# Single maxima of a two-branch attention kernel, spread over all steps by a running share

## The chip, the cores and the metric

The kernel runs on one core of a Trainium2 chip. The metric is device time in microseconds (us) of one execution, the median of several runs.

## The reference

Two attention branches over one input x (2048 rows, 512 columns), mixed row by row by a sigmoid gate:

```python
g = sigmoid((x * gate_w).sum(-1, keepdims=True))
a = A(x, wqkv, wo_a)      # 32 heads of 16; each row sees 8 rows: itself, 2, 4, .. 14 before
b = B(x, wq, wk, wv, wo_b)   # 32 heads of 16, one shared key and value head, all 2048 rows
return g * a + (1 - g) * b

# B, for each head: scores = q @ k.T / 4 ; p = softmax(scores) ; o = p @ v
```

The weights `B_wq` and `B_wk` are drawn eight times larger than the others, so B's scores are large, and its softmax needs the maximum of each row of scores before the exponential.

## The kernel before, in words

**Branch B** bounds the kernel. Its 32 *units* are 4 blocks of 512 query rows times 8 groups of 4 heads. A unit has 16 *steps*, one for each 128 keys, so there are 512 attention steps (`NS`). Step `s` takes four score matmuls on TensorE, in two pairs (`exp_pair`, line 569; a pair uses the upper and the lower 64 rows of the array side by side), into two PSUM buffers of two banks each, `pe0` and `pe1`. ScalarE takes the exponential of each buffer (line 571, `pexp`). One step later four matmuls multiply the exponentials with the values (`weighted`, line 579) and add up in the bank `po`.

The exponential needs the row maximum. It is subtracted inside the score matmul: two extra rows of the stacked queries `qst` hold it. So each unit's **maxima** must be known before its first step: 64 tasks a unit, each a score matmul with the queries as stationary side and 512 keys as moving side, and a reduction over them. There are 2048 such tasks (`NF`). They are taken in three ways:

- a *pair* (`fill_pair`): two matmuls side by side into the two-bank buffer `m2` (named `pm`), and one VectorE reduction of 1024 values (line 414). Most steps take one pair, between their two pairs of scores.
- a *single* (`fill_one`): one matmul into the bank `m1` (named `ps`), and one VectorE reduction of 512 values (line 425). A step takes at most one, and none in the first step of most units. The rule `singles` decides.
- *halves* (`fill_diff`, `fill_sum`, line 481): four maxima at once from sum and difference of two blocks of keys, with four matmuls, two absolute values on ScalarE and two fused reductions on VectorE (line 524). They are taken only where TensorE streams a projection on the other half of its rows.

`to_go()` is the number of maxima still to take. A finished unit of maxima goes through `filled`, `maxima_turn`, `shift_a` to `shift_d`: one closing reduction and a transpose on VectorE, small products, and eight small DMAs into `qst`. Units of queries are loaded into `qst` (`stack`) when a buffer comes free, so maxima can be taken only some units ahead: `stacked` lists the units loaded, and `home(v)[1]` is the unit that must be over before unit `v` can be loaded.

**The front** comes before the attention steps: the input's split into high and low parts, keys, queries, and branch A's projection in 48 pieces (line 1190). Maxima are taken along the way, in the end as halves.

**Branch A** runs on GpSimd (POOL) beside the attention steps, by a generator (`work`) that the planner feeds.

**Output rows** (branch A's and B's products with `wo_a`, `wo_b`) are made in two *output phases* (`out_phase`, line 863) of 8 and 4 rows between attention steps, each at the second step of a unit, with halves beside the products. The second phase starts when the lead in maxima falls under three units. The last 4 rows' products (line 934) are spread over the last steps (`spread`), once at most 9 maxima are left to take. They use `m2`, so no pairs go beside them.

**The order** of all this is fixed when the program is built. A planner in the kernel's own code keeps a clock for each engine (`clk`), due times of the banks (`free`) and a list of tasks, and writes the instructions in the order that comes out. Within a step the order is: first scores, pair, then second scores and single, or single and second scores where the planner thinks that the second score buffer is still held, then the weighted products.

Of the kernel before, what the change touches and what calls it, by code (L numbers as in the profile page):

```python
# [18 lines left out]
NJ = S // P  # L19
# [5 lines left out]
NU = NQB * NHG  # L25
# [10 lines left out]
NB = 8  # L36
NS = NU * NJ
NF = 2 * NU * 2 * 4 * 4
FMAX = 3.4028234e38
NH = NJ // 2  # L40
TO_END = 10
LAND = 3
LEAD, M2S, M1S, E1S, PER_ROW = 3.0, 0.5, 0.3, 0.2, 21
M2H = 0.15
WB = 6
# [33 lines left out]
def gated_mix_kernel(ctx, tc, xt, wa, wk, wq, wo_a, wo_b, out):  # L79
# [21 lines left out]
    def home(v):  # L101

        return (v % NB, v - NB) if v < 2 * NB - 2 else ((v - NB) % (NB - 2), v - NB + 2)
# [241 lines left out]
    stacked, asked = [], set()  # L345

    def stack(u):
        qb, hg = divmod(u, NHG)
        for b in range(2):
            hi, lo = (qd[s, :, qb, 4 * hg + 2 * b:4 * hg + 2 * b + 2, :].rearrange("d c n -> d (c n)") for s in range(2))  # L350
            ap = [list(x) for x in hi.ap]
            twice = bass.AP(tensor=hi.tensor, offset=hi.offset, ap=[ap[0], [0, 2]] + ap[1:])
            dst = qst[home(u)[0]].rearrange("p c n -> p (c n)").bitcast(F32)
            nc.sync.dma_start(dst[64 * b:64 * b + 32], twice)
            nc.sync.dma_start(dst[64 * b + 32:64 * b + 48], lo)
        stacked.append(clk["pe"] + 5.0)


    mx, left = {}, {}
    slots = [(v, pr, t, kc) for kc in range(2) for v in range(2) for pr in range(2) for t in range(4)]  # L360
    slots += [(v, pr, t, kc) for v in range(2) for pr in range(2) for t in range(4) for kc in range(2, 4)]
    slots += [(v, pr, t, kc) for v in range(2, NU) for pr in range(2) for t in range(4) for kc in range(4)]
    half = []
# [4 lines left out]
    def fillable():  # L368
        return bool(half) or bool(slots) and slots[0][0] < len(stacked) and stacked[slots[0][0]] <= clk["pe"]
# [17 lines left out]
    def to_go():  # L387
        return 2 * len(slots) + len(half)
# [41 lines left out]
    sel, kcd, dd, formed, ended, wants = [], [], [], set(), set(), []  # L430
# [40 lines left out]
    def half_back():  # L471

        nc.sync.dma_start(q67.rearrange("p g x n -> p (g x n)").bitcast(F32), kd.rearrange("p g x n -> p (g x n)"))
        kcd[0] = q67

    def paired():
        return len(slots) > 1 and slots[0][3] % 2 == 0 and slots[0][3] // 2 in formed and slots[1] == slots[0][:3] + (slots[0][3] + 1,) and fillable()
# [5 lines left out]
    groups, pend, half_free = [], [[], []], [0.0, 0.0]  # L483

    def diff_ready(odd):

        if max(half_free) != free["m2"]:
            half_free[:] = [free["m2"]] * 2
        if half_free[odd] > clk["pe"] or clk["dve"] - 1.6 > clk["pe"]:
            return False  # L490
        mine = [g for g in groups if odd in g[2]]
        if not mine and (groups or half or ended or wants or not paired()):
            return False
        d = mine[0][1] if mine else dd[0]
        return all(x[1] is not d for x in pend[odd])
# [66 lines left out]
    pe, pexp, exped = [], {}, {}  # L562
# [174 lines left out]
    def prepare(j, n, copy=None):  # L737
        nonlocal pool
        hi, lo = turned[j, 1] = [pe[0].tile([P, C, P], F32R, name=f"own{x}", bufs=1) for x in range(2)]
        own = ob[j // 4][:, :n, j % 4 * P:(j % 4 + 1) * P]  # L740
        if copy:
            copy(hi[:, :n], own)
            at = max(clk["pe"], pool / 1e3) + 1.3
        else:
            nc.scalar.activation(hi[:, :n], own, AF.Copy)
            at = after("act", clk["pe"], 0.6)
        nc.gpsimd.tensor_sub(lo[:, :n], own, hi[:, :n].bitcast(F32))
        pool = max(pool, 1e3 * at) + 1300
# [25 lines left out]
    def blocks_out(j):  # L774

        own = p2[0].tile([P, D], F32, name="raw", bufs=1)
        for k in range(2):
            nc.vector.transpose(own[:, k * D // 2:(k + 1) * D // 2], oa[k][:, j, :])
        after("dve", 0, 0.9)
        tasks.append((clk["dve"] + 0.3, blocks_in, (j, own)))  # L780
# [191 lines left out]

    def singles(s):

        if len(stacked) < NU:
            ready = len(half) + 2 * sum(x[0] < len(stacked) for x in slots[:16 * NB])
            if ready < 2 * (16 * (home(len(stacked))[1] + 1) + LAND - s) + 1:
                return False
        return 2 * max(0, 16 * (NU - 1) - 16 - s) + PER_ROW * max(0, NJ - 4 - outs) < to_go()

    def fill_ready(key, slack):
        if fillable() and free[key] <= clk["pe"] + slack:
            clk["pe"] = max(clk["pe"], free[key])
            if key == "m1":
                fill_one()
            elif half and (not slots or slots[0][0] >= len(stacked) or stacked[slots[0][0]] > clk["pe"]):
                fill_one(m2[:, 0, :], "m2")
            elif slots:
                fill_pair(m2, "m2")

    def pause(most):
        n = 0
        while n < most and slots and fillable():
            key = min(("e0", "e1", "m2"), key=lambda k: free[k])
            clk["pe"] = max(clk["pe"], free[key])
            if half:
                fill_one({"e0": eb[0], "e1": eb[1], "m2": m2}[key][:, 0, :], key)
                n += 1
                continue
            fill_pair({"e0": eb[0], "e1": eb[1], "m2": m2}[key], key)  # L1000
            n += 2
        return n
# [28 lines left out]
    def run_tasks():  # L1031
        for task in [t for t in tasks if t[0] <= clk["pe"]]:
            tasks.remove(task)
            task[1](*task[2])
# [207 lines left out]
    outs, due = 0, []  # L1242
    for s in range(NS + 1):
        u, kt = divmod(s, NJ)
        if s == 16 * NB + 4:
            half_back()
        if len(stacked) < NU and s >= 16 * (home(len(stacked))[1] + 1):
            stack(len(stacked))
        if s < NS and kt == 0 and u not in shifted:
            while u not in shifted:  # L1250
                clk["pe"] += 0.5
                run_tasks()
                if u not in shifted and left.get(u, 1):
                    assert pause(4)
        v = min(x[0][0] for x in (half, slots, [(NU,)]) if x)
        need = left.get(v, NF // NU)
        steps = 16 * v - 6 - s
        short = need - 2.8 * max(0, steps) if v < NU else 0
        lead = (NF - to_go()) / 64 - s / 16
        order = (0, "m2", "later") if s else ()  # L1260
        rows = 4 if outs else 8
        k, n = (outs + rows) // 4 - 1, C - (outs >= NJ - 4)
        if outs == NJ - 4:
            if s in (16 * NU - 40, 16 * NU - 32):
                blocks_out(outs + (s - 16 * NU + 40) // 8)
            if to_go() <= 9 and not later_rows and "last" not in done:
                later_rows.append(spread(list(range(outs, NJ)), n))
            if short > 0 and steps < 2:
                pause(short)
        elif due or outs < NJ and s and kt == 0 and outs // NH in done and NHG * (k + 1) - 1 in shaped and (lead < LEAD or s >= 16 * (NHG * (k + 2) + 1)):  # L1270
            if not due:
                prepare(outs, n)
                due.append(n)
            else:
                out_phase(list(range(outs, outs + rows)), due.pop(), kt == 1)
                outs += rows
                order = (0, "m1", 2)
        elif short > 0 and steps < 2:
            pause(short)

        first = 0
        some = min(4, -(-(row_prods[0] - TO_END) // (NS + 1 - s)))
        order = list(order)
        while order:
            which = order.pop(0)
            if which == "later":
                order = ["m1", 1] if free["e1"] > clk["pe"] - E1S else [1, "m1"]
                first = 0
            elif which == "m2":
                fill_ready("m2", M2S)  # L1290
            elif which == "m1":
                if not later_rows and (kt or not s or u >= NU - 8) and singles(s):
                    first = half[0][4] if half else 0
                    fill_ready("m1", M1S)
            elif s < NS:
                if which == 1:
                    spread_some(some)
                exp_pair(s, which % 2 or which // 2, which == 2, first)
        if s == NS:
            spread_some(some)  # L1300
        if s:
            weighted(s - 1)
            if kt == 0 and s < NS:
                finish_a(u - 1, nc.gpsimd)
        run_tasks()
        run_pool()
# [65 lines left out]
```

## Time and profile before

| what | value |
| --- | --- |
| time, median of 3 runs | 1473.9 us (1473.9 to 1474.03) |
| the profiled execution | 1473.35 us, span 1471.6 us |
| granted TensorE clock | 1.000 |
| front (until the first exponential of an attention step) | 268.65 us |
| singles in the front, in the attention steps (line 425) | 50, 374 |
| pairs (line 414) | 506 |
| steps 0 to 15, 176 to 191, 432 to 447 | 32.87, 33.82, 32.15 us |

The span runs from the first to the last instruction; the execution's time is a little longer. An exponential in a step starts ScalarE's row of line 571, so the steps' starts can be read from them. A busy time of TensorE is modelled from the starts of pipelined matmuls, so it reads as full also where an instruction waits a little between two others.

### The profile page before, as it was taken

To read this page: it belongs to the slowest core of one execution; us is meant where nothing else is said; L and a number is where in the kernel's file an instruction comes from. 1 tells how busy PE (TensorE), PEld (TensorE's weight loads), DVE (VectorE), ACT (ScalarE), POOL (GpSimd) and SP (SyncE) were. 2 spreads that over 40 slices of the span, in tenths; PEclk is the share of its full clock that TensorE was granted. 3 is DMA by queue.
4 is the path that set the end of the run, shared out by engine and by line. 5 is a ranking of instruction groups with operands and counts; after the bars stand their busy time and mean duration, and the time that the engine had idled before them with its cause. 6 is when DMAs were issued, how large, how long until landed. Compare 5 with 4: busy or idle time off the path is not lost.

```text
span 1471.6 us, 28990 instructions
## 1 busy us (share of the span) xinstructions
PE 1461.3 (99%) x10612; PEld 669.0 (45%) x10612; DVE 1189.9 (81%) x1865; ACT 1288.7 (88%) x1629; POOL 1003.5 (68%) x1753
## 2 busy tenths in 40 slices
PE   9999999999999999999999999999999999999998
PEld 5877777433333333333333376333333336433343
DVE  6978889688888988889898888889898887766612
ACT  5658888999999999999999978999999998999986
POOL 7853888878898988888888888788888213101221
PEclk9999999999999999999999999999999999999999
DMA  6752533222121110211211202021120000000110
GB/s 224 211 162 74 147 92 100 74 56 77 29 88 42 45 65 36 71 42 42 71 41 41 82 23 86 22 72 42 42 71 12 12 13 26 16 1 2 29 32 29
DMA packets 75263, 89.80 MB, mean 61 GB/s; under 512 B 56368, under 2 KB 56416, under 8 KB 70896
## 3 DMA queue, kind: packets, MB, share of 16 engines
q1 hardware_dynamic: 68176, 49.00, 11.8%
q0 software_dynamic: 6368, 37.90, 7.8%
q8 instruction: 83, 1.36, 0.4%
q10 hardware_dynamic: 576, 1.05, 0.2%
q14 instruction: 60, 0.49, 0.1%
HBM read 60.03 MB, written 27.35 MB: 59 GB/s over the span
## 4 chain that ended last, share of the span: by engine, by line
PE 95%; DVE 2%; POOL 1%; issue 1%; ACT 1%; DVEq 0%; POOLq 0%; ACTq 0%
PE po L579 35%; PE pe L569 24%; PE pe L1190 10%; PE pm L385 8%; PE ps L385 6%; PE pe L863 4%; PE pm L481 2%; PE ps L481 2%; PE po L481 2%; PE pm L934 1%; PE pe L209 1%; DVE qst L187 0%; POOL wal L113 0%; DVE pexp L524 0%; POOL qlo L255 0%
## 5 line engine op out<-in xcount | busy, mean ns | idle before, releaser
L571 ACT ACTIVATE pexp<-pe 128x1024 f32<-128x1024 f32 x1022 | 989.8, 1022 | 84.5 <-PE pe L569 78.9
L414 DVE TENSOR_REDUCE mx<-pm 128x2 f32<-128x1024 f32 x506 | 619.1, 1223 | 152.1 <-PE pm L385 147.4
L579 PE MATMUL po<-pexp,vst 128*32 128x512 f32 x4096 | 545.5, 605 | 0.0
L569 PE MATMUL pe<-qst,kst 64*128 64x512 f32 x1916 | 440.4, 453 | 0.2
L569 PEld LDWEIGHTS pe<-qst,kst 64*128 64x128 f32 x1916 | 179.7, 183 | 482.2 <-ACT pexp L571 477.1
L425 DVE TENSOR_REDUCE mx<-ps 128x1 f32<-128x512 f32 x399 | 271.5, 680 | 0.6 <-PE ps L385 0.6
L385 PE MATMUL pm<-kst,qst 62*128 62x512 f32 x978 | 196.8, 395 | 0.3 <-DVE mx L414 0.3
L643 POOL TENSOR_TENSOR pr<-aext 128x256 f32<-128x256 f32 x256 | 182.8, 741 | 4.7 <-DMA aext<-ad 4.4
L703 POOL TENSOR_TENSOR oa<-oa,av 128x256 f32<-128x256 f32 x224 | 164.4, 734 | 14.9
L579 PEld LDWEIGHTS po<-pexp,vst 128*32 128x32 f32 x4096 | 80.5, 108 | 169.2 <-issue 160.7
L385 PE MATMUL ps<-kst,qst 62*128 62x512 f32 x397 | 157.2, 396 | 0.2 <-DVE mx L425 0.2
L700 POOL TENSOR_TENSOR av<-aext,lg 128x256 f32<-128x256 f32 x224 | 139.6, 623 | 12.9
L507 ACT ACTIVATE dd<-pm 128x512 f32<-128x512 f32 x186 | 105.0, 606 | 23.2 <-PE pm L481 15.3
L1190 PE MATMUL pe<-wah,xh 64*128 64x512 f32 x376 | 119.9, 397 | 0.1
L1190 PE MATMUL pe<-wal,xh 64*128 64x512 f32 x376 | 118.4, 395 | 0.8 <-POOL wal L113 0.8
L1190 PE MATMUL pe<-wah,xl 64*128 64x512 f32 x376 | 118.8, 395 | 0.0
L385 PEld LDWEIGHTS pm<-kst,qst 62*128 62x128 f32 x978 | 94.3, 187 | 2.9 <-DVE mx L414 0.9
L606 POOL TENSOR_TENSOR rl<-rl,gate_t 128x16 f32<-128x16 f32 x31 | 6.9, 223 | 128.0 <-DVE rl L600 126.8
L649 POOL TENSOR_TENSOR tr<-pr 128x512 f32<-128x512 f32 x64 | 81.8, 1278 | 4.2
L507 ACT ACTIVATE pexp<-pm 128x512 f32<-128x512 f32 x120 | 68.5, 608 | 14.5 <-PE pm L481 8.2
L649 POOL TENSOR_TENSOR tr<-tr 128x256 f32<-128x256 f32 (+1 forms) x128 | 72.6, 567 | 8.7
L524 DVE CUSTOM_DVE_ANT_0 dd<-ps,dd 128x512 f32<-128x512 f32 x93 | 64.2, 690 | 15.8 <-PE ps L481 8.7
(214 smaller groups left out, 1983.3 us busy)
## 6 DMA issues: line engine op xcount, KB each, us to landing
aext<-ad POOLq DMA_DIRECT2D x32, 1056.0 KB, 5.5
qst<-qd SPq DMA_DIRECT2D x60, 128.0 KB
ad<-stage SPq DMA_DIRECT2D x32, 240.0 KB
xraw<-xt SPq DMA_DIRECT2D x16, 256.0 KB
qd<-qhi SPq DMA_DIRECT2D x16, 256.0 KB
qd<-qlo SPq DMA_DIRECT2D x16, 256.0 KB
qst<-qd SPq DMA_DIRECT2D x60, 64.0 KB
qst<-ml SPq DMA_DIRECT2D x216, 2.0 KB
```

Of the source, the lines that this page charges most:

```text
L385: nc.tensor.matmul(dst, qst[home(v)[0]][b:b + 62, pr, t * P:(t + 1) * P], kst[b:b + 62, kc * 512:(kc + 1) * 512], start=True, stop=True)
L414: nc.vector.tensor_reduce(m[:, :, pr, t, kc], dst, AX.X, ALU.max)
L425: nc.vector.tensor_reduce(m[:, odd, pr, t, kc:kc + 1], dst, AX.X, ALU.max)
L507: nc.scalar.activation(d[:, odd], m2[:, odd, :], AF.Abs)
L569: nc.tensor.matmul(bank[:, odd, :], kst[b:b + 64, kt * P:(kt + 1) * P], qst[home(u)[0]][b:b + 64, pr, :], start=True, stop=True)
L571: nc.scalar.activation(e, bank, AF.Exp, scale=SCALE)
L579: nc.tensor.matmul(po[32 * i:32 * i + 32, :], vst[:, kt, :], pexp[s, i // 2][:, i % 2, :], start=(kt == 0), stop=(kt == NJ - 1))
L643: nc.gpsimd.tensor_mul(pr[:, k], q, e[:, o:o + NH, AC:2 * AC])
L649: nc.gpsimd.tensor_add(nx, cur[:, :, 0:n], cur[:, :, n:2 * n])
L700: nc.gpsimd.tensor_mul(av, e[:, o:o + NH, 2 * AC:].rearrange("p j (h d) -> p j h d", d=DH), lg[:, w].unsqueeze(3).to_broadcast([P, NH, AG, ...
L703: nc.gpsimd.tensor_add(ao, ao, av)
L1190: nc.tensor.matmul(front[2 if x == last else x % 2][0][:, b, :], l[h], r[h], start=(i == 0), stop=(i == 3 * C - 1))
```

## The change

Three things are changed.

1. `singles` was a threshold. While more maxima were left than two for each step to come (and 21 for each output row to come), every step took a single; after that none did. Now each step adds a share to an account (`single_share`): what is left beyond those pairs, divided by the steps to come, at most 1. A single is taken when the account holds 1.
2. While units of queries are still to be loaded, the share is also held to what is loaded already: the maxima ready, divided by the steps until the next unit's queries are there, less 2 for the pairs. Before, a step took no single at all unless enough maxima were ready.
3. The front starts no new group of halves once 468 maxima are taken (`FRONT`).

```diff
+FRONT = 468
...
-        if not mine and (groups or half or ended or wants or not paired()):
+        if not mine and (groups or half or ended or wants or not paired() or not pe and NF - to_go() >= FRONT):
             return False
...
     def singles(s):
 
-        if len(stacked) < NU:
-            ready = len(half) + 2 * sum(x[0] < len(stacked) for x in slots[:16 * NB])
-            if ready < 2 * (16 * (home(len(stacked))[1] + 1) + LAND - s) + 1:
-                return False
-        return 2 * max(0, 16 * (NU - 1) - 16 - s) + PER_ROW * max(0, NJ - 4 - outs) < to_go()
+        most = to_go() - 2 * max(0, 16 * (NU - 1) - 16 - s) - PER_ROW * max(0, NJ - 4 - outs)
+        if most <= 0 or share[0] < 1.0:
+            return False
+        share[0] -= 1.0
+        return True
+
+    def single_share(s):
+
+        left = 16 * (NU - 1) - 16 - s
+        if left > 0:
+            most = to_go() - 2 * left - PER_ROW * max(0, NJ - 4 - outs)
+            rate = most / left
+            if len(stacked) < NU:
+                ready = len(half) + 2 * sum(x[0] < len(stacked) for x in slots[:16 * NB])
+                wait = 16 * (home(len(stacked))[1] + 1) + LAND - s
+                rate = min(rate, ready / wait - 2)
+            share[0] = min(2.0, share[0] + max(0.0, min(1.0, rate)))
+        else:
+            share[0] = 1.0
+
+    share = [0.0]
...
+        single_share(s)
         while order:
```

The built order shows what becomes of it. In its rows a line number of the changed kernel is one higher than before for the same statement of branch B (L569 is L570, L385 is L386, L579 is L580, L481 is L482), and line 1190 is line 1207. `pe_85` and `pe_86` are the two score buffers, `pm` is `m2`, `ps` is `m1`; the queries of a unit are in `qst` or `q`.

The first place is the end of the front on TensorE. `wah`, `wal`, `xh`, `xl` are branch A's projection, `kcd` the halves' keys. Before:

```order
L1190 MATMUL pe_86<-wah,xl 128x512
L481 MATMUL pm<-kcd,q_76 128x512
L1190 MATMUL pe_86<-wah,xl 128x512
L1190 MATMUL pe_86<-wah,xh_109 128x512 x2
L481 MATMUL ps<-kcd,q_76 128x512
L1190 MATMUL pe_86<-wal,xh_109 128x512 x2
L1190 MATMUL pe_86<-wah,xl 128x512 x2
L1190 MATMUL pm<-wah,xh_108 128x512
L481 MATMUL po<-kcd,q_76 128x512
L1190 MATMUL pm<-wah,xh_108 128x512
L1190 MATMUL pm<-wal,xh_108 128x512 x2
```

The same place now:

```order
L1207 MATMUL pe_86<-wah,xh_109 128x512 x2
L1207 MATMUL pe_86<-wal,xh_109 128x512 x2
L1207 MATMUL pe_86<-wah,xl 128x512 x2
L1207 MATMUL pm<-wah,xh_108 128x512 x2
L1207 MATMUL pm<-wal,xh_108 128x512 x2
L1207 MATMUL pm<-wah,xl 128x512 x2
```

The front's last two groups of halves (eight matmuls of line 481, with their reductions and absolute values) are gone, and the projection's matmuls stand in twos, one for each half of the rows.

The second place is on TensorE in the middle, step 121. Before, as in the 14 steps around it:

```order
L569 MATMUL pe_85<-q_76,kst 128x512 x2
L385 MATMUL pm<-kst,qst_81 128x512 x2
L569 MATMUL pe_86<-q_76,kst 128x512 x2
L385 MATMUL ps<-kst,qst_81 128x512
L579 MATMUL po<-pexp,vst 32x512 x4
```

Steps 121 and 122 now:

```order
L570 MATMUL pe_85<-q_76,kst 128x512 x2
L386 MATMUL pm<-kst,qst_81 128x512 x2
L570 MATMUL pe_86<-q_76,kst 128x512 x2
L580 MATMUL po<-pexp,vst 32x512 x4
L570 MATMUL pe_85<-q_76,kst 128x512 x2
L386 MATMUL pm<-kst,qst_81 128x512 x2
L386 MATMUL ps<-kst,qst_81 128x512
L570 MATMUL pe_86<-q_76,kst 128x512 x2
L580 MATMUL po<-pexp,vst 32x512 x4
```

One step in four or five has lost its single, and in the step behind it the single stands ahead of the second scores.

The third place is late, on TensorE, steps 408 and 409. Before:

```order
L569 MATMUL pe_85<-qst_82,kst 128x512 x2
L385 MATMUL pm<-kst,qst_79 128x512 x2
L569 MATMUL pe_86<-qst_82,kst 128x512 x2
L385 MATMUL ps<-kst,qst_79 128x512
L579 MATMUL po<-pexp,vst 32x512 x4
L569 MATMUL pe_85<-qst_82,kst 128x512 x2
L385 MATMUL pm<-kst,qst_79 128x512 x2
L569 MATMUL pe_86<-qst_82,kst 128x512 x2
L579 MATMUL po<-pexp,vst 32x512 x4
```

The same two steps now:

```order
L570 MATMUL pe_85<-qst_82,kst 128x512 x2
L386 MATMUL pm<-kst,qst_79 128x512 x2
L386 MATMUL ps<-kst,qst_79 128x512
L570 MATMUL pe_86<-qst_82,kst 128x512 x2
L580 MATMUL po<-pexp,vst 32x512 x4
L570 MATMUL pe_85<-qst_82,kst 128x512 x2
L386 MATMUL pm<-kst,qst_79 128x512 x2
L570 MATMUL pe_86<-qst_82,kst 128x512 x2
L386 MATMUL ps<-kst,qst_79 128x512
L580 MATMUL po<-pexp,vst 32x512 x4
```

Before, step 408 has the last single but one; from step 409 to step 480 one single is left. Now singles go on, four or five in six steps, up to step 475. The second output phase, which stood at step 417, stands at step 401.

## The prediction

> **What bounds the kernel now.** I read the page's engine totals first, then a table of stages, then the waits of ScalarE in two stages, and last the order in time on TensorE. The page:
>
> ```profile
> PE 1461.3 (99%) x10612; PEld 669.0 (45%) x10612; DVE 1189.9 (81%) x1865; ACT 1288.7 (88%) x1629; POOL 1003.5 (68%) x1753
> ```
>
> TensorE looks full everywhere, so this row cannot tell which steps have slack. The table of stages can. Its rows give the stretch, its length, then the busy time of PE, of weight loads (PEld), DVE, ACT and POOL. I cut three stretches of sixteen attention steps each: steps 0 to 15, then steps 176 to 191, then steps 432 to 447.
>
> ```profile
> 268.65:301.52 32.87, 32.72 (x231) 11.65 (x227) 18.64 (x20) 31.44 (x34) 25.78 (x43) 1.00 0.25 72
> 640.85:674.67 33.82, 33.82 (x243) 12.12 (x241) 29.68 (x35) 31.18 (x34) 30.98 (x51) 1.00 0.25 80
> 1292.51:1324.66 32.15, 32.15 (x226) 10.29 (x224) 20.42 (x18) 31.03 (x33) 0.84 (x2) 1.00 0.00 1
> ```
>
> The same stretches for line 425 alone, the VectorE reduction that each single maximum ends in:
>
> ```profile
> 640.85:674.67 33.82, 10.21 (x15) 1.00 0.25 80
> 1292.51:1324.66 32.15, 0.00 (x0) 1.00 0.00 1
> ```
>
> So the middle stretch has 15 singles and the late one none, yet PE reads as full in both. A stretch with no single takes 32.15 / 16 = 2.009 us a step. Now who waits. ScalarE's waits in a stretch of fifteen singles like the middle one (369.55 to 403.39) are one row (who waited for whom, total us, times, longest):
>
> ```profile
> ACT pexp L571 <- PE pe L569: 2.7, 14, 0.2
> ```
>
> In both late stretches without singles (1292.51 to 1356.81) the same view has no row: ScalarE never waits there long enough to be listed. With singles TensorE sets the pace and ScalarE waits about 0.2 us at nearly every step. Without them ScalarE's exponentials, and the two score banks that they free, set it. The order in time on TensorE gives the price of each kind of step; a step runs from one first pair of scores (L569 ahead of the L385 pair) to the next:
>
> ```profile
> 705.75 0.50 PE L569 MATMUL pe<-qst,kst 64*128 64x512 f32 x2
> ...
> 707.89 0.50 PE L569 MATMUL pe<-qst,kst 64*128 64x512 f32 x2
> ...
> 709.78 0.50 PE L569 MATMUL pe<-qst,kst 64*128 64x512 f32 x2
> 710.12 0.39 PE L385 MATMUL pm<-kst,qst 62*128 62x512 f32 x2
> 710.35 0.39 PE L385 MATMUL ps<-kst,qst 62*128 62x512 f32 x1
> 710.49 0.50 PE L569 MATMUL pe<-qst,kst 64*128 64x512 f32 x2
> ...
> 711.91 0.50 PE L569 MATMUL pe<-qst,kst 64*128 64x512 f32 x2
> ```
>
> The step from 705.75 has a single and takes 2.14. The step from 707.89 is a unit's first step, where singles are barred: it takes 1.89. The next has its single ahead of the second pair of scores (710.35) and takes 2.13. So one lone step without a single gives its whole matmul back, 2.13 - 1.89 = 0.24. In a run of such steps it doesn't:
>
> ```profile
> 1299.94 0.49 PE L569 MATMUL pe<-qst,kst 64*128 64x512 f32 x2
> ...
> 1301.99 0.50 PE L569 MATMUL pe<-qst,kst 64*128 64x512 f32 x2
> ...
> 1303.95 0.49 PE L569 MATMUL pe<-qst,kst 64*128 64x512 f32 x2
> ```
>
> Here steps take 2.05 and 1.96, the 2.009 of the stage table. The instructions on TensorE are those of the 1.89 step. The difference, 0.119, is time in which TensorE waits for a bank that ScalarE still reads. The kernel before spends its singles early and leaves three long runs without them.
>
> **The change part by part.** The sum is made against the profiled execution's own time, 1473.35 us (span 1471.6); the median of the three timed runs, 1473.9, lies 0.55 above it, and the result is moved up by that. All counts are from the order of the two built kernels. Both have the same 8542 instructions in TensorE's order, so no work goes away; what moves is where a maximum is taken.
>
> *Singles spread.* Outside the output phases, attention steps up to 484 are 369 with a single and 108 without before, 372 and 106 now. Of the 108, 85 stood in runs (steps 2 to 16, 409 to 416, 419 to 480) and 23 alone. Of the 106, 12 stand in runs (three pairs and one run of six) and 94 alone, and nearly every lone one is followed by a single ahead of the second scores, as in the row at 710.35. So 73 steps change from 2.009 to 1.89: 73 x 0.119 = **-8.7 us**. The price of a lone step is not seen away from a unit's start. From above it is bounded by the run's 2.009 (gain nothing), from below by the 1.89 row. I take 1.89, because the row's neighbours have the very order that the change makes.
>
> *Three more singles* in the steps: 3 x 0.24 = **+0.7**, as those steps are paced by TensorE.
>
> *The front* loses its last two groups of halves, that is eight matmuls. They run beside a projection on the other half of the rows, one slot apart:
>
> ```profile
> 263.79 0.39 PE L481 MATMUL po<-kcd,q 62*128 62x512 f32 x1
> 263.80 0.38 PE L1190 MATMUL pe<-wah,xh 64*128 64x512 f32 x1
> 264.02 0.39 PE L481 MATMUL pm<-kcd,q 62*128 62x512 f32 x1
> 264.03 0.39 PE L1190 MATMUL pe<-wal,xh 64*128 64x512 f32 x1
> ```
>
> A slot is 0.23, and each lone matmul fills half of one: 4 x 0.23 = **-0.9**. The bound on the other side is zero, if ScalarE's copies of the last projections end it instead. The eight maxima of these groups come back in steps 2 to 16: nine singles where there were none. That is priced above.
>
> *The first output phase* (step 273 in both) takes one group more, four half slots: **+0.5**. The second moves from step 417 to step 401 with the same 42 half matmuls on the difference and as many on the sum. Its products need branch A's last rows from POOL. POOL's last such product before, and the phase's first matmul:
>
> ```profile
> 1146.95 0.74 POOL L703 TENSOR_TENSOR oa<-oa,av 128x256 f32<-128x256 f32 x1
> ...
> 1224.21 0.73 PE L863 MATMUL pe<-woh,own 64*128 64x512 f32 x2
> ```
>
> The cover is 77 us. It loses 16 steps of 2.1 and the gain so far (some 42 in all), and the planner issues POOL's last product eight or nine steps later than before (up to 19), so about 16 are left. If it were gone, each us that POOL is late would be a us on the path. I cost it at nothing.
>
> *The last row's products.* The output rows that are spread over the end start at step 481 and not 480, so three of their 84 slots move into steps that TensorE paces. A slot there:
>
> ```profile
> 1393.10 0.39 PE L934 MATMUL pm<-woh,turned 64*128 64x512 f32 x2
> 1393.33 0.63 PE L934 MATMUL pm<-wol,turned 64*128 64x512 f32 x4
> ```
>
> 3 x 0.23 = **+0.7**, or nothing if the step given up was not hidden either.
>
> *What else moves.* A single is one matmul and one VectorE reduction; no DMA goes with it. A unit's turned maxima (small DMAs on SP and POOL) are issued when its last maximum is taken, which is now later in most units. Counted from the order, the maxima are still at least 2.38 units ahead of the steps at the tightest point before the late stage (2.53 before), some 79 us at 33.8 a unit, so nobody waits for them. VectorE gets less to do per step where it was fullest.
>
> Sum: -8.7 + 0.7 - 0.9 + 0.5 + 0.7 = -7.7. So 1473.35 - 7.7 = 1465.65 for a profiled run, and **1466.2** as a median.
>
> **The rivals.** *A: lone steps are not cheaper when they are dense (same).* The 1.89 was seen once in sixteen steps; with one in five, the loop through the two score banks (scores, exponential, next scores) may hold two steps at 2 x 2.009 = 4.02. Against it: a lone step and its successor together take 1.89 + 2.13 = 4.02 already, so the loop is just kept; for it: there is no slack to spare. If the 73 steps cost 2.009 as before, -8.7 falls away and the small terms stay: 1473.9 + 0.7 - 0.9 + 0.5 + 0.7 = 1474.9. The Trainium skill, page "Perfetto Trace Analysis", section "Identifying the Most-Contended Engine", leaves matmul busy time out as a measure and names the engine of highest occupancy as the one to work on. By that rule ScalarE's 88% is the limit here, and moving matmuls between steps would leave the time as it is. The rows agree with the page on the busy time (full in both stages), but ScalarE's share is 31.18 of 33.82 in the middle stage and 31.03 of 32.15 late: it binds in one of them alone. Chance 0.10.
>
> *B: half of it.* Lone steps between 1.89 and 2.009, at 1.95: half of 8.7 is lost, 1470.5. Chance 0.07.
>
> *C: slower, by VectorE's backlog at the single's bank.* A single writes its bank only after VectorE has reduced the one before. Where VectorE had a unit's closing reduction to do, that came late:
>
> ```profile
> 1050.81 0.50 PE L569 MATMUL pe<-qst,kst 64*128 64x512 f32 x2
> ...
> 1051.66 0.49 PE L385 MATMUL ps<-kst,qst 62*128 62x512 f32 x1
> ...
> 1053.08 0.49 PE L569 MATMUL pe<-qst,kst 64*128 64x512 f32 x2
> ```
>
> This step takes 2.27, 0.14 over the usual 2.13. The change puts 96 singles ahead of the second scores, where 25 were; there a late bank holds up the scores as well. At 0.14 for each of the 96 it adds 13.4, and 1466.2 becomes 1479.6. It decides from 7.7 / 96 = 0.08 a step. Against it: the single at 710.35 is exactly this case, and its step took 2.13; and a step without a single gives VectorE 0.68 less to do just before. Chance 0.07.
>
> That the change doesn't do what it says is excluded by the order: the spread and the two missing groups are in it.
>
> **How the numbers follow.** The forecast has 0.76 and lies between 1463 and 1469: the lower end if steps like the one at 1050.81 (I count ten with a single over 2.2, at 0.14 each some 1.4 us) vanish as well and two of the small costs are hidden, the upper if a quarter of the 8.7 and the front's 0.9 are lost. B's 0.07 lies above it. The range 1463.0 to 1472.0 holds these two less a little at the ends, 0.8; A and C lie outside. A difference of 0.2%, 2.9 us, is about what a measurement of this kernel can tell from none. Faster by more than that: 0.76 + 0.07 = 0.83. Within it: A, 0.10. Slower: C, 0.07.
>
> **What would show it right or wrong.** In the trace after: late stretches of sixteen steps with 13 singles at about 13 x 2.13 + 3 x 1.89 = 33.4 (before: 32.15 with none), middle ones at 33.4 (before 33.82); steps 0 to 15 about 0.5 longer; the first score matmul of attention about 0.9 earlier; ScalarE's waits for TensorE in every unit. It is wrong if lone steps take 2.0 (A or B), if steps with the single ahead take over 2.2 (C), or if the second output phase starts with a wait for POOL.

## The result, and the profile after

| | before | after |
| --- | --- | --- |
| median of five runs each | 1473.9 us | 1468.02 us (1467.86 to 1468.92) |
| ratio, 95% interval | | 0.9961 (0.9946 to 0.9975) |
| the profiled execution | 1473.35 us | 1468.92 us |
| its span | 1471.6 us | 1467.1 us |

The kernel is faster by 5.9 us in the medians; 7.7 was forecast (1466.2, range 1463.0 to 1472.0). The profiled execution, from which the parts below come, is one of the longer ones: it gained 4.4.

First the same row of engine totals. TensorE is as full as before, though 4.4 us went:

```profile
PE 1454.0 (99%) x10612; PEld 675.4 (46%) x10612; DVE 1191.7 (81%) x1864; ACT 1285.3 (88%) x1627; POOL 1001.2 (68%) x1753
```

Then the table of stages (columns as before: stretch, length, PE, PEld, DVE, ACT, POOL, clock) for steps 0 to 15, 176 to 191 and a late stretch, steps 448 to 463:

```profile
267.43:300.47 33.04, 33.04 (x240) 13.19 (x236) 23.22 (x26) 31.39 (x36) 25.93 (x51) 1.00 0.22 67
637.09:670.42 33.33, 33.33 (x240) 12.11 (x238) 28.50 (x35) 31.04 (x34) 26.82 (x59) 1.00 0.13 44
1317.08:1350.49 33.41, 33.41 (x241) 12.16 (x240) 29.16 (x35) 30.89 (x33) 3.84 (x9) 1.00 0.01 2
```

The same stretches for the single's reduction alone (line 426 now):

```profile
267.43:300.47 33.04, 5.45 (x8) 1.00 0.22 67
637.09:670.42 33.33, 8.17 (x12) 1.00 0.13 44
1317.08:1350.49 33.41, 8.85 (x13) 1.00 0.01 2
```

So singles are spread: 8, 12 and 13 where the three stretches of before had none, 15 and none. The middle one went from 33.82 to 33.33, and the late one takes 33.41 with its 13; 33.4 was forecast for both. The first stretch is 0.17 longer, where 0.5 was forecast. ScalarE now waits for TensorE in the late stretch too (waits, 1317.08 to 1350.49):

```profile
ACT pexp L572 <- PE pe L570: 2.7, 14, 0.2
```

A lone step without a single and the step behind it, late in the kernel, in order of time on TensorE:

```profile
1326.91 0.50 PE L570 MATMUL pe<-qst,kst 64*128 64x512 f32 x2
...
1328.81 0.50 PE L570 MATMUL pe<-qst,kst 64*128 64x512 f32 x2
1329.15 0.40 PE L386 MATMUL pm<-kst,qst 62*128 62x512 f32 x2
1329.38 0.39 PE L386 MATMUL ps<-kst,qst 62*128 62x512 f32 x1
1329.51 0.50 PE L570 MATMUL pe<-qst,kst 64*128 64x512 f32 x2
...
1330.93 0.50 PE L570 MATMUL pe<-qst,kst 64*128 64x512 f32 x2
```

1.90, and then 2.12 with the single ahead of the second scores: the price that the forecast rests on, some 620 us later in the kernel than where it was read.

**What had not been foreseen** stands at step 19, again on TensorE, with the idle time and its releaser in brackets:

```profile
306.22 0.49 PE L570 MATMUL pe<-qst,kst 64*128 64x512 f32 x2
306.56 0.39 PE L386 MATMUL pm<-kst,qst 62*128 62x512 f32 x1
308.33 0.47 PE L386 MATMUL pm<-kst,qst 62*128 62x512 f32 x1 [1.39 <-DMA qst<-qd]
308.34 0.70 PE L570 MATMUL pe<-qst,kst 64*128 64x512 f32 x2
308.68 0.39 PE L386 MATMUL ps<-kst,qst 62*128 62x512 f32 x1
308.99 1.66 PE L580 MATMUL po<-pexp,vst 128*32 128x512 f32 x8
310.58 0.79 PE L570 MATMUL pe<-qst,kst 64*128 64x512 f32 x2
...
313.63 0.50 PE L570 MATMUL pe<-qst,kst 64*128 64x512 f32 x2
```

The pair's second matmul waits 1.39 for the queries of unit 8, whose maxima begin here. Behind the wait everything is slow: the weighted products take 1.66 where 1.06 is usual. The table of stages for these microseconds shows the granted clock (third value from the end) at half:

```profile
309.00:310.00 1.00, 1.00 (x10) 0.15 (x8) 1.00 (x2) 0.92 (x1) 1.00 (x3) 0.66 0.02 8
310.00:311.00 1.00, 1.00 (x6) 0.42 (x4) 0.66 (x2) 0.10 (x1) 1.00 (x3) 0.50 0.00 0
311.00:312.00 1.00, 1.00 (x6) 0.74 (x5) 0.15 (x1) 0.52 (x1) 0.84 (x4) 0.50 0.00 0
312.00:313.00 1.00, 1.00 (x7) 0.20 (x8) 1.00 (x2) 1.00 (x2) 1.00 (x3) 0.63 0.01 2
```

The two steps take 4.36 and 3.05 and not 2.13 each: 3.15 us lost. Before, the same pair, also in step 19, started later and without a listed wait:

```profile
307.61 0.53 PE L385 MATMUL pm<-kst,qst 62*128 62x512 f32 x2
```

Its two matmuls start at 307.61 and 307.67, with no idle time to speak of. Four loads on SP's queue bring them. Here are the first of them and branch A's load of 1 MB (`aext`), before:

```profile
298.90 0.59 POOL L632 DMA_DIRECT2D aext<-ad  x1
299.99 0.62 SPq L354 DMA_DIRECT2D qst<-qd  x1
```

And after, the first, branch A's load, then the third and the fourth, whose issue takes 1.61 where its neighbour's takes 0.58:

```profile
298.94 0.61 SPq L355 DMA_DIRECT2D qst<-qd  x1
299.68 0.59 POOL L633 DMA_DIRECT2D aext<-ad  x1
300.28 0.58 SPq L355 DMA_DIRECT2D qst<-qd  x1
300.90 1.61 SPq L356 DMA_DIRECT2D qst<-qd  x1
```

The need moved 1.05 ahead, from 307.61 to 306.56, since the front ends 1.2 earlier. The queries' first load is issued 1.05 earlier as well, but their last packet ends at 306.83 before and at 306.96 after: from the first issue to the last packet the four loads take 8.02 and not 6.84. Branch A's load, which was issued 1.1 ahead of the first of them, now comes between them. From the last packet to the pair's second matmul, 0.84 pass before and 1.37 after; why, no run here shows.

By stages the profiled execution changed so: front 268.65 to 267.43, -1.22; steps 0 to 479 without the output phases 1005.72 to 1001.86, -3.86, with the 3.15 of the wait in it; the output phases' steps 75.79 to 75.18 and 38.80 to 39.36, together -0.05; from step 480 on 82.61 to 83.30, +0.69.

### The profile page after: what moved, and what is told of

Same layout as the page of the kernel before. It is cut to its first block, busy times and chain, and to the rows that moved or that the text cites. A ratio compares the mean times of both kernels' runs of the same rounds, so it can differ in the third digit from the quotient of the medians.

```text
span 1467.1 us, 28988 instructions
## 1 busy us (share of the span) xinstructions
PE 1454.0 (99%) x10612; PEld 675.4 (46%) x10612; DVE 1191.7 (81%) x1864; ACT 1285.3 (88%) x1627; POOL 1001.2 (68%) x1753
## 3 DMA queue, kind: packets, MB, share of 16 engines
q10 hardware_dynamic: 576, 1.05, 0.2%
## 4 chain that ended last, share of the span: by engine, by line
PE 94%; DVE 2%; POOL 1%; DMA 1%; issue 1%; ACT 1%; DVEq 0%; POOLq 0%; SPq 0%; ACTq 0%
PE po L580 34%; PE pe L570 23%; PE pe L1207 10%; PE pm L386 8%; PE ps L386 6%; PE pe L864 4%; PE pm L482 3%; PE po L482 2%; PE ps L482 2%; PE pm L935 1%; PE pe L210 1%; DMA xraw<-xt 1%; DMA qst<-qd 0%; POOL wal L114 0%; DVE mx L415 0%
## 5 line engine op out<-in xcount | busy, mean ns | idle before, releaser
L580 PE MATMUL po<-pexp,vst 128*32 128x512 f32 x4096 | 546.1, 605 | 0.2 <-DVE tt L594 0.2
L570 PE MATMUL pe<-qst,kst 64*128 64x512 f32 x1916 | 442.6, 451 | 0.0
L570 PEld LDWEIGHTS pe<-qst,kst 64*128 64x128 f32 x1916 | 179.8, 183 | 473.8 <-ACT pexp L572 468.1
L386 PE MATMUL pm<-kst,qst 62*128 62x512 f32 x981 | 198.3, 396 | 2.0 <-DMA qst<-qd 1.4
L580 PEld LDWEIGHTS po<-pexp,vst 128*32 128x32 f32 x4096 | 80.6, 108 | 164.8 <-issue 155.4
L386 PE MATMUL ps<-kst,qst 62*128 62x512 f32 x390 | 154.3, 396 | 0.2 <-DVE mx L426 0.2
L386 PEld LDWEIGHTS pm<-kst,qst 62*128 62x128 f32 x981 | 94.5, 186 | 5.9 <-DMA qst<-qd 1.8
```

Of the source, the lines that this page charges most:

```text
L386: nc.tensor.matmul(dst, qst[home(v)[0]][b:b + 62, pr, t * P:(t + 1) * P], kst[b:b + 62, kc * 512:(kc + 1) * 512], start=True, stop=True)
L570: nc.tensor.matmul(bank[:, odd, :], kst[b:b + 64, kt * P:(kt + 1) * P], qst[home(u)[0]][b:b + 64, pr, :], start=True, stop=True)
L580: nc.tensor.matmul(po[32 * i:32 * i + 32, :], vst[:, kt, :], pexp[s, i // 2][:, i % 2, :], start=(kt == 0), stop=(kt == NJ - 1))
```

## The experiments

The theory after the result: a step without a single gives back its whole 0.24 where it stands alone, and about half where such steps stand in runs; against that stands a new wait at step 19. The rivals: the gain comes from the front; it comes from fewer singles; order inside a step doesn't matter; a single ahead of the second scores costs something of its own (rival C). Each group of four ran on one chip, beside its own runs of before.

**Singles in clusters.** The account is as in the change, but singles start when it holds four and stop when it is under one. By the trace, of the 106 steps without a single outside the output phases, up to step 484, 85 now stand in runs, most of them runs of four, and 21 alone.

```diff
-        if most <= 0 or share[0] < 1.0:
+        if share[0] >= 4.0:
+            share[1] = 1.0
+        elif share[0] < 1.0:
+            share[1] = 0.0
+        if most <= 0 or not share[1]:
```

> The changed kernel, but the account is let grow to 4 before singles start, and they go on until it is under 1: as many singles in the attention steps (373 for 372), in blocks, so that 40 single-less steps follow another one (6 in the changed kernel, 42 before). Theory (a single-less step gives its matmul back only where it stands alone; behind another one it costs 2.12 in place of 1.89): 34 x 0.23 = 7.8 us more than the changed kernel, about 1475.8 us. Rival (only the number of singles counts, or the missing groups of the front): about 1468.

Measured: 1475.57 us, ratio 1.0014 (1.0005 to 1.0023). The number of singles is that of the kernel after within one, the front's stop is in both, and a wait at step 19 with the slow clock behind it is in both profiles. The spacing differs, and the whole gain is gone: in the profiles the steps outside the output phases take 1009.53 against 1001.86, 7.7 more. That it is spacing that pays is shown.

**The spread alone**, without the front's stop:

```diff
-        if not mine and (groups or half or ended or wants or not paired() or not pe and NF - to_go() >= FRONT):
+        if not mine and (groups or half or ended or wants or not paired()):
```

> The spread without the front's stop at 468. Theory: the front gets its 0.9 us back, the output phases lose three groups of halves (1.4 less), two singles and two single-less followers more (0.9): 1468.4 us, if the wait for unit 8's queries at step 19 stays, and 1466 to 1467 if that goes. Rival (the front's stop brings the gain): 1473 or more.

Measured: 1466.58, ratio 0.9951 (0.9938 to 0.9965): at least as much as the whole change brings (0.9961, on another chip; the intervals overlap). Step 19 still waits there, but less and at full clock:

```profile
308.34 0.47 PE L386 MATMUL pm<-kst,qst 62*128 62x512 f32 x1 [0.47 <-DMA qst<-qd]
```

**The front's stop alone**, with the old rule for singles:

> The kernel before with the front's stop at 468 and nothing else. Theory: 0.9 less in the front, seven singles more (1.7) and three single-less followers fewer (0.7 less): 1474.0 us, no change. Rival (the front's stop brings the gain): 1468 to 1471.

Measured: 1474.86, ratio 1.0009 (1.0000 to 1.0018). The front ends at 267.96 in its profile, some 0.7 earlier than before, but the eight maxima come back in the steps, and step 19 waits 0.79 for the same loads, which makes it 1.06 longer and is most of the 1.3 that this kernel lies above before. The front brings none of the gain.

**The wait taken away.** The planner counts unit 8's queries 1.5 us later, so it takes their maxima later:

```diff
-        stacked.append(clk["pe"] + 5.0)
+        stacked.append(clk["pe"] + (6.5 if len(stacked) == NB else 5.0))
```

> The changed kernel, but the planner counts unit 8's queries as there 1.5 us later, so step 19 takes no pair and the first matmul on them comes a step (2 us) later; one more group of halves and three more single-less followers come with it (some 1.0 us). Theory (the changed kernel loses 2 to 3 us at step 19 to the late queries and to the slower clock behind the wait): 1466.0 to 1467.0 us, and no step over 2.5 us near 306 us. Rival (the wait is only in the profiled execution, or comes back a step later): 1468.5 to 1469.

Measured: 1466.15, ratio 0.9951 (0.9938 to 0.9963). No wait for a DMA is left at step 19 and the clock stays full. The edit does a little more than take the wait away, as the expectation says: it also moves a group of halves and some singles. Both kernels were then run side by side on another chip:

> The kernel after, unchanged, on the chip of the next three, since the kernel with the moved load came out at 1467.39 on another chip than the one with the later queries (1466.15). 1468.0 to 1469.0; the wait of step 19 and the slow clock behind it are there in most executions.

> Unit 8's queries counted 1.5 us later, once more. Theory (the wait with its slow clock costs about 2): 1.5 to 2.5 below the kernel after on this chip. Rival (the 1.9 between the two came from the chips): within 0.5 of it.

Measured: after 1467.37 (1466.85 to 1469.27), ratio 0.9957 (0.9944 to 0.9969); with the later queries 1466.16 (1465.95 to 1466.98), ratio 0.9948 (0.9935 to 0.9960). The gain was 1.2, less than the 1.5 to 2.5 expected, and the profile of after on this chip says why:

```profile
306.40 0.50 PE L570 MATMUL pe<-qst,kst 64*128 64x512 f32 x2
306.74 0.40 PE L386 MATMUL pm<-kst,qst 62*128 62x512 f32 x1
308.14 0.47 PE L386 MATMUL pm<-kst,qst 62*128 62x512 f32 x1 [1.00 <-DMA qst<-qd]
308.14 0.69 PE L570 MATMUL pe<-qst,kst 64*128 64x512 f32 x2
308.48 0.40 PE L386 MATMUL ps<-kst,qst 62*128 62x512 f32 x1
308.81 1.06 PE L580 MATMUL po<-pexp,vst 128*32 128x512 f32 x8
309.80 0.50 PE L570 MATMUL pe<-qst,kst 64*128 64x512 f32 x2
```

The wait is 1.00, the weighted products behind it take 1.06, and the step takes 3.40: 1.27 lost and not 3.15. So a wait of 1.00 costs 1.27 at full clock; a wait of 1.39 would cost about 1.7 by the same measure (an estimate: 0.39 more), and the slow clock behind it in the first profile the other 1.5. How often the clock falls can be bounded from the mean granted clock of each run. 3.4 us at half rate lower the mean of 1466 us to 0.9988, so a run that shows 1.000 had no such fall: these are three of the five runs of after on the first chip, its median run among them, and three of the five here. The run at 1469.27, 1.9 above the median, shows 0.998; the four runs on record with 0.998, of three kernels, are each the longest of their kernel or next to it. So the fall is in at most four of these ten executions, where it had been expected in most.

**The colliding load moved.** Branch A's generator hands the planner 6 us more before this load, so that no 1 MB load runs beside the queries:

```diff
+            if i == 0:
+                yield 6000
             yield from load(i + 2)
```

> After, with branch A's first 1 MB load in the attention steps put off by 6 us of the planner's clock, so that it no longer runs beside the load of unit 8's queries; TensorE's order keeps the same number of singles, pairs and halves. Theory (the queries come late at step 19 because the two loads share the DMA engines): the wait of step 19 and the slow clock behind it go, 1466.0 (1465.7 to 1466.8), like the kernel whose planner counts these queries 1.5 us later (1466.15). Rival (the queries' own transfer is too slow, whatever runs beside it): step 19 still takes over 4 us, 1468.0.

Measured: 1467.39, ratio 0.9958 (0.9944 to 0.9972): not the 1466.0 of the theory. On the chip of the last pair:

> Branch A's load moved, once more. Theory: within 0.5 of the kernel with the later queries on the same chip. Rival (the load's place has a price of its own in the front or later): 0.5 to 1.5 above it.

Measured: 1467.45 (0.9956, 0.9942 to 0.9970), 1.3 above the kernel with the later queries, as the rival has it. Yet the wait is gone: step 19 takes 2.12 in both profiles, and no wait of TensorE for a DMA is listed. The stage table from 302 to 305, of after and then of the kernel with the moved load (second value from the end: share of the DMA engines):

```profile
302.00:305.00 3.00, 3.00 (x26) 1.44 (x22) 2.75 (x5) 2.66 (x4) 0.19 (x1) 1.00 0.93 357
```

```profile
302.00:305.00 3.00, 3.00 (x25) 1.02 (x23) 2.74 (x4) 2.85 (x4) 2.69 (x5) 1.00 0.29 83
```

With the big load out of the way the DMA engines are at 0.29 and not 0.93, and the queries' last packet ends at 304.51 and not 306.96, though the first of these loads was issued 1.0 later: 4.55 us after it and not 8.02. That the queries are late because other loads run beside them is shown. But the edit moved more than the text above says: two loads of 256 KB on SP's queue (`os<-wo_a`), issued at 302.89 in after, start at 315.41 here. Their packets run from 304.73 in after, beside the last of the queries', so what part of the delay is theirs was not separated. What eats the gain is elsewhere: this kernel's front ends at 268.39 and 268.30 in its two profiles, against 267.55 and 267.53 with the later queries, and the rest is spread over the steps and the end. Why the moved load lengthens the front was not followed.

**The order inside the step**, two kernels. All singles ahead of the second scores:

```diff
-                order = ["m1", 1] if free["e1"] > clk["pe"] - E1S else [1, "m1"]
+                order = ["m1", 1]
```

> After, with every single ahead of the second scores: 388 such steps and not 106. The planner then takes 17 singles more in the steps and some halves fewer in the output phases. Theory (a single ahead costs its own matmul, 0.24, and nothing else): 1468.0 + 17 x 0.24 - about 2 = 1470 (1468.5 to 1471.5). Rival C of the prediction (VectorE's backlog at the single's bank then holds up the scores, 0.14 a step): 1468 + 282 x 0.14 = 1507; it is still alive at 1475 and above.

and all behind them (`order = [1, "m1"]`):

> After, with every single behind the second scores: 72 steps with a single follow a step without one in that order, 3 in the kernel after. 21 singles more in the steps (+5.0), fewer halves in the output phases (about -2.8). Theory (a step without a single gives back its 0.24 only if the next step's second scores come late, since the second score buffer is held by ScalarE; with them first the next step takes 2.36 to 2.40 and the gain is lost): 1468.0 + 2.2 + 69 x 0.24 = 1487 (1482 to 1490). Rival (only the spacing counts, not the order inside the step): 1470.

Measured: all ahead 1479.03, ratio 1.0036 (1.0022 to 1.0050); all behind 1486.53, ratio 1.0087 (1.0074 to 1.0101). The second is as the theory has it. A step without a single and the next, in the kernel with all behind:

```profile
378.73 0.50 PE L570 MATMUL pe<-qst,kst 64*128 64x512 f32 x2
...
380.63 0.50 PE L570 MATMUL pe<-qst,kst 64*128 64x512 f32 x2
380.96 0.40 PE L386 MATMUL pm<-kst,qst 62*128 62x512 f32 x2
381.32 0.50 PE L570 MATMUL pe<-qst,kst 64*128 64x512 f32 x2
381.67 0.40 PE L386 MATMUL ps<-kst,qst 62*128 62x512 f32 x1
...
382.99 0.50 PE L570 MATMUL pe<-qst,kst 64*128 64x512 f32 x2
```

1.90 and then 2.36. The loads of weights for the two pairs of scores in this step tell who holds them (timeline of weight loads):

```profile
380.62 0.19 PEld L570 LDWEIGHTS pe<-qst,kst 64*128 64x128 f32 x2 [0.84 <-ACT pexp L572]
...
381.32 0.18 PEld L570 LDWEIGHTS pe<-qst,kst 64*128 64x128 f32 x2 [0.35 <-ACT pexp L572]
```

The second scores come when ScalarE still reads their bank. With the single in that gap nothing is lost; behind them it is added.

All singles ahead falls between the theory's and the rival's number, nine above the theory. Its waits, 480 to 620, have a row that the same stretch of after lacks:

```profile
PEld ps L386 <- DVE mx L426: 7.8, 36, 0.6
```

That is rival C's wait: the single's bank is still held by VectorE's reduction of the single before. The steps' lengths, grouped by what stood in the step before (medians of the distances between ScalarE's first exponentials, with counts), show where it bites:

| step | step before it | before | after | all ahead | all behind |
| --- | --- | --- | --- | --- | --- |
| no single | single | 1.90 (26) | 1.90 (97) | 1.90 (81) | 1.90 (74) |
| no single | no single | 2.04 (81) | 2.09 (6) | 2.11 (6) | 2.10 (9) |
| single behind the second scores | single | 2.13 (339) | 2.13 (270) | | 2.13 (316) |
| single ahead | no single | 2.13 (23) | 2.13 (93) | 2.13 (79) | |
| single ahead | single | 2.17 (3) | 2.19 (3) | 2.17 (306) | |
| single behind the second scores | no single | | 2.36 (3) | | 2.36 (72) |

A single ahead costs 0.035 more behind a step with a single, and nothing behind a step without one. 306 such steps make 10.7 us, about the nine that were missing. In the kernel after there are three.

The second row mixes two lengths. In a run of steps without a single, short and long ones alternate: the first to the fourth of a run take 1.90, 2.12, 1.91 and 2.11 in the kernel with clusters (medians of 21, 21, 21 and 18 steps), and in the 60 steps of before from 420 on 1.95 and 2.06 take turns. So it is every second step of a run that gives nearly nothing back, and the mean of a run is the 2.01 of the prediction's stage table.

**Two attempts to use this.** One takes the later queries, a single always ahead behind a step without one, and a single at a unit's last step while any is left:

> A version made from the findings: after, with unit 8's queries counted 1.5 us later, a single always ahead of the second scores behind a step without one, and a single at a unit's last step whenever any is left (so that its first step, where none is taken, is a lone one). Against the kernel with the later queries alone (1466.15): 8 pairs of neighbouring steps without a single fewer (about -1.0), one single behind the second scores after a lone step fewer (-0.2), four more singles (+1.0). Theory: 1465.9 (1465.2 to 1466.6). Rival (runs of two cost nothing against lone steps): 1467.

Measured: 1467.75, ratio 0.9960 (0.9947 to 0.9972), above the theory's range. No better, and not clearly worse, as the kernel with the later queries did not run on that chip. In the profiles its steps outside the output phases take 999.69 against 999.04: the four more singles seem to cost at least what the eight fewer neighbouring steps gave. The other has the later queries and one rule for the order:

```diff
-                order = ["m1", 1] if free["e1"] > clk["pe"] - E1S else [1, "m1"]
+                order = ["m1", 1] if s - 1 not in taken else [1, "m1"]
```

> The later queries, and the order inside the step by one rule: the single ahead of the second scores exactly where the step before took none. Against the later queries alone it has no step with the single ahead behind a step with one (7 there, 0.035 each), 2 steps fewer in pairs without a single and one single more: about 0.2 below it, which this comparison can hardly tell from none. If it is over 1 above, the price list of the steps (1.90 lone, 2.13, 2.17 ahead behind a single, 2.36 behind the second scores after a lone step) lacks something.

Measured: 1466.31, ratio 0.9948 (0.9936 to 0.9961), the same as the later queries alone. Those remain the best version: 1466.15 and 1466.16 on two chips.

## Why the prediction was right, and where it was not

**Singles spread, -8.7 and +0.7.** Right in mechanism, and nearly in size. Lone steps take 1.90 in all stretches, so rivals A and B are refuted. The steps outside the output phases lost 3.86, and without the 3.15 of step 19 they lost 7.0, where 8.0 was forecast. Three singles that still stand behind the second scores after a lone step lose 0.23 each, which would be 0.7 of the missing 1.0; the prediction passed over them with "nearly every lone one".

**The front, -0.9.** -1.22 in the profile, -1.08 in the second profile of the same kernel. But it was no gain in the end: alone it made the kernel 1.3 slower than its neighbouring runs of before, some 1.06 of it by the wait at step 19.

**The output phases, +0.5 and nothing.** -0.61 and +0.56; both signs missed, the sum small. The cover of POOL's rows was held: its last product starts at 1153.58 and the second phase's first matmul at 1180.12, 26 us later, where 16 were reckoned, and no wait of TensorE for POOL is listed there.

**The last rows, +0.7.** +0.69 from step 480 on.

**"Nobody waits": the step that failed.** The prediction counted how far the finished maxima are ahead of the steps that use them, 2.38 units (some 80 us at 33.8 a unit, not 79), and concluded that nobody waits. It did not count the other end: how soon after a unit's queries land they are first needed for the next maxima. From the last packet to the pair of step 19 that was 0.78 before (306.83 to 307.61), which was enough, and is -0.40 after (306.96 to 306.56). Both the issue of the loads and the need moved 1.05 ahead; the landing didn't. Branch A's load, issued by another engine on its own schedule, now falls between these loads, and they take 1.2 longer (the last section sets the transfer times of all kernels side by side; what part the two loads of 256 KB have stays open). The term that is missing is the wait: 1.27 where it was 1.00 at full clock, and 3.15 in the profiled execution, where the clock fell behind it.

The sum of the other terms holds: with the wait taken away the kernel is 7.78 below before on the same chip (1473.94 to 1466.16), and 7.37 on another, where -7.7 was forecast. On the chip of the 7.78 the kernel after is 6.57 below, so there the wait is the whole miss (1.21 between the two kernels). On the first chip, where the median's miss is 1.8, the two did not run side by side. That the sum came out so near is in part luck: in the profiled execution, without the 3.15, the singles brought 1.0 less than forecast, the front 0.3 more and the output phases 0.5 more.

**Rival C** was real, but its place was wrong. It was priced from a closing reduction of VectorE at 0.14 for every single ahead of the second scores. It is 0.035, and only behind a step with a single; the change puts its singles ahead where VectorE has just had a step with less to do.

**The rule in rival A.** The measurement is 5.9 us less, with ScalarE's busy share at 88% in both profiles. The rule that the prediction took from the Trainium skill, page "Perfetto Trace Analysis", section "Identifying the Most-Contended Engine", names the engine to work on first; read as rival A read it, it would have left the time as it was. Of the same page of the Trainium skill the section "Optimization Strategy" says that where the most contended engine changes over time, interleaving the regimes may help. That agrees with these runs: stretches paced by TensorE (2.13 a step) and stretches paced by ScalarE (2.01) were mixed, and putting the same singles back into clusters gave the gain back.

## What to carry to other kernels

Where two engines are nearly balanced, slack work is worth its full time only if it is dealt out so that each engine's short step meets the other's long one; read the price of a lone short step and of a run of them separately. A change that makes a stretch earlier moves its loads against those that other engines issue: for every load of that stretch compare the time of its landing with the time of its first use, before and after, and not only the lead of the results. And the order inside a step decides whether a saved slot is kept.

## What the runs showed of the hardware

A short wait can cost a second time through the clock. After 1.39 us of waiting the granted clock stood at 0.50 from about 309.3 to 312.7 (the rows for 309 to 313 above, 0.66 and 0.63 taken as part 1.00 and part 0.50), which cost about 1.5 of the 3.15 us (an estimate, from the 1.27 that a wait of 1.00 cost at full clock). Waits of 0.47, 0.79, 1.00 and 1.16 us at the same place, in other kernels and other chips, left it at 1.00 (1.00 is the second run of the same kernel). But in the kernel with clusters the clock also fell behind two gaps of 0.62 and 0.44 with one matmul between them:

```profile
310.00:311.00 1.00, 1.00 (x10) 0.18 (x4) 0.56 (x1) 0.60 (x1) 0.84 (x3) 0.52 0.00 0
311.00:312.00 1.00, 1.00 (x6) 0.80 (x7) 0.00 (x0) 0.28 (x1) 1.00 (x3) 0.50 0.00 0
```

So the length of one wait alone doesn't decide it; what does was not settled. The Trainium skill, page "TensorE: Matmul & The Clock Gate", section "HAM oscillation — how this bites in real kernels", gives gaps of over about 3.4 us as the rule for when the clock falls. The half rate agrees with these rows, and so does the length of the slow stretch, 3.4 us, the window that this section of the Trainium skill names; the length of the gap before it does not.

What a large load does to small ones beside it depends on the order of issue. The four loads of unit 8's queries (384 KB together, on SP's queue) took 4.46 and 4.55 us from their first issue to their last packet with no other load near; 6.84 and 6.96 where branch A's 1 MB load was issued more than 1 us ahead of the first of them (before, and the spread alone); and 7.5 to 8.3 in the ten other profiles, where it was issued from 0.2 ahead of the first to 1.1 behind it. In the last two groups the two loads of 256 KB follow as well. The issue of the fourth load on SP's queue took 1.27 to 1.78 in the seven profiles in which the large load was issued 0.07 to 0.42 behind the second, and 0.58 in all others, where it was issued ahead of the second or some 7 us later.
